# A later start of the weight rounding, with moved reciprocals, decay copies and buffers, in a fused attention and feed-forward kernel

## The chip, the cores and the metric

The kernel runs on one core of a Trainium2 chip. The metric is the device time of one execution in microseconds (us). The core has five engines that run side by side, each with its own in-order queue: TensorE (PE) for matrix products, VectorE (DVE), ScalarE (ACT) and GpSimd (POOL) for elementwise work, and SyncE (SP), which here issues nearly all of the DMA transfers. An instruction that waits holds up everything behind it on its own engine.

## The reference

The reference is an attention with a decay and a causal mask, followed by a feed-forward layer. B = 8 batches, H = 8 heads, S = 576 positions, D = 64 values per head, model width 512, hidden width 2048.

```python
scores = scale * np.matmul(q, k.transpose(0, 1, 3, 2))
cum = np.cumsum(np.log(np.clip(f, 0.0001, 1.0)), axis=-1)
scores = np.where(causal, -1e9, scores + cum[:, :, :, None] - cum[:, :, None, :])
attn = np.exp(scores - np.max(scores, axis=-1, keepdims=True))
attn = attn / (np.sum(attn, axis=-1, keepdims=True) + 1e-09)
x = np.matmul(attn, v)              # then heads are laid side by side: [4608, 512]
h = x @ w_in                        # [512, 2048]
g = np.maximum(h, 0.0) + alpha * np.minimum(h, 0.0)
out = g @ w_out                     # [2048, 512]
```

All of it is in fp32. The kernel splits each factor of a product into a rounded high part and a rest, and takes three products for one.

## The kernel before

**Attention** goes by pairs of heads: 32 pairs, n = 0 to 31, four to a batch. For each pair PE multiplies the query and key parts (`stretch`, and `tail` for the last 64 rows), DVE adds the decay rows `Z` and takes the row minimum (L744, L620), ACT takes the exponential and the row sum (L579), the result is transposed, and PE multiplies it with the values (`values`, `prods_of`).

- Pairs 0 to 9 transpose on PE (L592) and move the result out of PSUM with `evac` (L587 on DVE, L588 on ACT).
- Pairs 10 to 31 are **turned**: DVE transposes 32x32 blocks from the buffer `E` into `M` (L754), and sixteen DMAs (L764, ten issued by SP and six by POOL) carry them into the buffer `TT`, from which the value product reads. There are two `M` buffers and one `TT` buffer, so the DMAs of a pair can start only when the value product of the pair before has read `TT`. The value product of a pair runs two pairs late (`behind`). In the profile's names `TT` is a part of the tile `wr`, and `E` and `M` are parts of the tile `big`.
- For a turned pair, DVE spreads the decay into `Z` (L483), POOL copies parts of it to two more places (L501 and L502, two of each to a pair) and adds the mask (L504). POOL also makes the rests of query and key (L538).
- `rqk` holds the raw query and key rows, loaded by SP (L471, or L474 and L475) and read by ACT (L537) and POOL (L538). Up to pair 10 it has two buffers; the turned pairs after that use a ring `rqk1` with one.
- `quotients` turns the row sums into reciprocals: ACT adds a small number (L670), DVE takes the reciprocal (L671), PE transposes (L673), ACT copies (L674), SP writes them to DRAM (`rd`, L679) and fetches them back spread over partitions (`ri`, L686). They multiply the value product (L844), after which x is rounded (L846) and its rest taken (L848).

**The first feed-forward product** (`ffn1`, L362 with `xx,wi`) needs x of a whole batch and the rounded first weight `wi`. That weight is rounded in 16 pieces by `split64`: loads (L343), ACT (L345, L357), DVE (L348, L349, L352, L353), POOL (L358). Its products fill the time on PE between the steps of attention. **The second** (`w_out`) runs alone at the end as a seven-product scheme.

**The order** on every engine is written out by a small list scheduler, `Plan`, at build time. Each operation has an engine, an estimated duration, a key and the buffers it needs; of those that could start first the one with the smallest key is taken. The first product's operations have keys around 1e6, so that they come where nothing of attention can start. Up to 75 us of the plan, a gap on PE of over 0.5 us is filled with products whose result nobody reads (`fill`, L456). `CONV0` and `CONV` give the keys of the 16 weight pieces: `CONV0 + CONV * fc`, where pair n has the keys around `10 * n`.

## Time and profile before

| | |
|---|---|
| median of 3 runs | 1046.42 us (1045.65 to 1049.57) |
| the profiled execution, its own time | 1045.14 us |
| its span, first to last instruction | 1043.3 us |
| mean granted TensorE clock | 0.995 |
| PE busy | 1028.2 us of the span |
| DVE, ACT, POOL busy | 802.0, 631.2, 403.8 us |

Busy time of PE is the union of its matrix products, with their ends modelled; products follow each other faster than one takes, so a count and a stretch of time tell more than the duration of one. "Idle before" an instruction is put down to the engine or the DMA whose signal came last. The granted clock is given as a share of the full one.

### The profile page before, as it was taken

What the parts mean: (1) busy time and instruction counts of PE and PEld (TensorE: products, weight loads), DVE (VectorE), ACT (ScalarE), POOL (GpSimd) and SP (SyncE); (2) the same over time, 40 slices, a digit from 0 to 9 for tenths busy, and PEclk for the clock granted to TensorE, in tenths of its full rate; (3) what the DMA queues carried; (4) which work ended last, traced back from release to release, by engine and by line L of the source; (5) the groups of instructions that cost most, each with busy time, mean ns of one, the idle gap of its engine ahead of it and who ended that gap; (6) DMA issues with size and microseconds to landing.
All of it is one profiled execution on the core that took longest, in us unless ns stands there. A gap on an engine that the chain in (4) does not pass through costs nothing.

```text
span 1043.3 us, 22505 instructions
## 1 busy us (share of the span) xinstructions
PE 1028.2 (99%) x7994; PEld 899.7 (86%) x7994; DVE 802.0 (77%) x1702; ACT 631.2 (61%) x1462; POOL 403.8 (39%) x719
## 2 busy tenths in 40 slices
PE   9999999998999999999999999999999999999998
PEld 5888888787887787887888888899999999999998
DVE  5786885886776776767742987599898888989994
ACT  6779896675666666656552665655464545546551
POOL 6487674878887888886641000000000000000000
PEclk9999999998999999999999999999999999999999
DMA  5876754676888778886776666463434335344411
GB/s 173 236 224 209 231 171 131 195 218 180 254 236 224 233 225 229 245 242 183 213 207 194 213 222 203 166 201 121 140 123 140 122 122 161 117 129 139 124 62 41
DMA packets 125230, 187.74 MB, mean 180 GB/s; under 512 B 20967, under 2 KB 70622, under 8 KB 125118
## 3 DMA queue, kind: packets, MB, share of 16 engines
q1 hardware_dynamic: 120606, 173.13, 54.6%
q0 software_dynamic: 4224, 12.98, 4.8%
q8 instruction: 63, 1.03, 0.4%
q14 instruction: 49, 0.40, 0.1%
q10 hardware_dynamic: 288, 0.20, 0.1%
HBM read 102.80 MB, written 48.52 MB: 145 GB/s over the span
## 4 chain that ended last, share of the span: by engine, by line
PE 88%; POOL 4%; DMA 3%; DVE 2%; SPq 1%; issue 1%; ACT 1%; DVEq 0%; ACTq 0%; POOLq 0%
PE bank L362 84%; PE bank L592 2%; DMA rqk<-in_qk_dram 2%; SPq L764 1%; POOL Z L504 1%; PE bank L422 1%; POOL Ql L538 1%; POOL Kl L538 0%; DMA rd<-R 0%; PE bank L632 0%; DMA hd<-hs 0%; DVE big L744 0%; PE bank L456 0%; POOL xs L844 0%; POOL Z L510 0%
## 5 line engine op out<-in xcount | busy, mean ns | idle before, releaser
L362 PE MATMUL bank<-xx,wi 128*128 128x512 f32 x1728 | 418.2, 395 | 0.7 <-ACT eT L633 0.7
L362 PEld LDWEIGHTS bank<-xx,wi 128*128 128x128 f32 x1728 | 317.6, 188 | 74.1 <-issue 3.8
L579 ACT ACTIVATE big<-big,st 128x384 f32<-128x384 f32 (+4 forms) x268 | 156.1, 585 | 16.6 <-DVE st L744 15.1
L930 DVE SCALAR_TENSOR_TENSOR hs<-bank,sa,hs 128x512 f32<-128x512 f32 x96 | 71.7, 747 | 93.3 <-ACT hs L928 93.0
L362 PE MATMUL bank<-wot,xx 128*128 128x256 f32 x1008 | 123.9, 283 | 0.0
L362 PE MATMUL bank<-wi,xx 128*128 128x256 f32 x1008 | 123.9, 283 | 0.0
L362 PEld LDWEIGHTS bank<-wot,xx 128*128 128x128 f32 x1008 | 122.3, 192 | 0.0
L362 PEld LDWEIGHTS bank<-wi,xx 128*128 128x128 f32 x1008 | 122.3, 192 | 0.0
L744 DVE CUSTOM_DVE_ANT_0 big<-bank,Z 128x384 f32<-128x384 f32 (+3 forms) x211 | 92.9, 485 | 31.0 <-PE bank L362 22.9
L928 ACT ACTIVATE hs<-bank,ab 128x512 f32<-128x512 f32 x96 | 65.9, 686 | 82.5 <-PE bank L362 76.2
L754 DVE STREAM_TRANSPOSE big<-big 128x1152 f32<-128x1152 f32 (+1 forms) x66 | 79.3, 1221 | 13.6 <-ACT big L579 11.3
L764 POOL DMA_DIRECT2D wr<-big x132 | 66.4, 508 | 44.1 <-PE bank L632 24.7
L362 PE MATMUL bank<-wr,vr 128*64 128x128 f32 (+1 forms) x1232 | 68.3, 266 | 6.0 <-DMA wr<-big 4.2
L362 PEld LDWEIGHTS bank<-wr,vr 128*64 128x64 f32 x1232 | 60.1, 141 | 13.7 <-issue 6.9
L504 POOL TENSOR_TENSOR Z<-Z,tri 128x128 f32<-128x128 f32 x176 | 70.7, 428 | 0.0
L1153 ACT ACTIVATE xx<-gx 128x1024 fp32r<-128x1024 f32 x48 | 50.8, 1058 | 30.7 <-PE bank L362 15.1
L848 POOL TENSOR_TENSOR xx<-xs,xx 128x256 fp32r<-128x256 f32 x64 | 48.1, 764 | 49.4 <-ACT xx L846 49.0
L1156 DVE TENSOR_TENSOR xx<-gx,xx 128x1024 fp32r<-128x1024 f32 x48 | 58.5, 1218 | 7.9 <-ACT xx L1153 7.9
L362 PE MATMUL bank<-wi,gh 128*128 128x256 f32 x504 | 62.4, 283 | 0.0
L362 PE MATMUL bank<-wot,gh 128*128 128x256 f32 x504 | 62.4, 283 | 0.0
L362 PEld LDWEIGHTS bank<-wot,gh 128*128 128x128 f32 x504 | 61.4, 192 | 0.1
L362 PEld LDWEIGHTS bank<-wi,gh 128*128 128x128 f32 x504 | 61.3, 192 | 0.0
(157 smaller groups left out, 1749.4 us busy)
## 6 DMA issues: line engine op xcount, KB each, us to landing
hd<-hs SPq DMA_DIRECT2D x144, 256.0 KB
wx<-hd SPq DMA_DIRECT2D x47, 512.0 KB
wr<-big SPq DMA_DIRECT2D x220, 96.0 KB
rqk<-in_qk_dram SPq DMA_DIRECT2D x28, 512.0 KB
hr<-hd SPq DMA_DIRECT2D x25, 512.0 KB
wr<-big POOLq DMA_DIRECT2D x132, 96.0 KB, 3.7
vr<-in_vv_dram SPq DMA_DIRECT2D x32, 320.0 KB
wr<-in_w_in_dram SPq DMA_DIRECT2D x16, 512.0 KB
```

Source lines behind the costliest of these rows:

```text
L362: pe.matmul(o, lhsT, rhs, start=start, stop=stop)
L504: ms.append(op("POOL", c_po(128), lambda to=to, i=i, zd=zd: po.tensor_tensor(to()[:, :, -1:], zd()[:, :, i : i + 1], tk(), ALU.add), kc + ...
L579: ex = op("ACT", c_exp(w), lambda: ac.activation(at(bt.t), at(bt.t), AF.Exp, bias=lo()[:, col : col + 1], scale=-1.0, accum_out=su()[:, co ...
L592: pe.transpose(t[:, c : c + 128], src[:, 128 * j : 128 * j + 128], ident)
L744: ve.tensor_tensor_reduce(out=o if turned else blk(o), in0=blk(bS.t[:, c0 : c0 + w]), in1=in1(), scale=-0.125, scalar=3.0e38, op0=ALU.add, ...
L754: ve.transpose(part(bm.t), part(bE.t))
L764: got.append(op(e_, 600, lambda a=a, k=k, q_=q_: q_.dma_start(bTT.t[32 * k : 32 * k + 32, 768 * a : 768 * a + 768], bm.t[32 * a : 32 * a + ...
L848: xl = op("POOL", c_po(256), lambda r=r, t0=t0: po.tensor_tensor(bx.t[:, 1, t0 : t0 + 256], bxs[r].t[:, 0:256], bx.t[:, 0, t0 : t0 + 256]. ...
L928: cp = op("ACT", c_act(512), lambda bh=bh, bs=bs, fc=fc: ac.activation(bs.t, bh.t, AF.Relu, scale=ab[:, fc : fc + 1]), -1000, [last, o_sg] ...
L930: cp = op("DVE", c_dve(512), lambda bh=bh, bs=bs, fc=fc: ve.scalar_tensor_tensor(bs.t, bh.t, sa[:, fc : fc + 1], bs.t, ALU.mult, ALU.add), ...
L1153: his.append(op("ACT", c_acs(128 * GW * (j1 - j0)), lambda j0=j0, j1=j1, src=src, o_=o_: ac.activation(o_(0, j0, j1), src(), AF.Copy), key ...
L1156: rdy.append(op("DVE", c_dve(128 * GW * (j1 - j0)), lambda j0=j0, j1=j1, src=src, o_=o_: ve.tensor_tensor(o_(1, j0, j1), src(), o_(0, j0, ...
```

## The change

- `CONV0, CONV` go from 30, 2.2 to 40, 2.0: the keys of the weight pieces go from 30 ... 63 to 40 ... 70.
- `quotients` of turned pairs gets a key that is 20 smaller, so that its steps go ahead of others that could start at the same time.
- The two copies L501 and L502 go from POOL to ACT for the turned pairs: 44 of each.
- `rqk` keeps two buffers to the end; `rqk1` is gone.
- The memory of `TT` and of one `M` buffer is exchanged: `TT` lies in `big` now, and one of the two `M` buffers in `wr`. The counts stay the same.
- A second copy of the decay table in DRAM, `c8p`, is written by five DMAs on SP. It would be read by turned pairs that fetch their decay by DMA; with NZ = NX[0] = 10 there is none, so nothing reads it.
- `PJ` names the same three of eight DMAs for POOL as before, and `2 * NZ` and `NZ` are the same numbers as `2 * NX[0]` and `NX[0]`.

```diff
@@ -41,4 +41,5 @@
 LAG = 1000
+PJ = (2, 4, 6)
 VK, TK = 0.65, 5
-CONV0, CONV = 30, 2.2
+CONV0, CONV = 40, 2.0
 NW = NF // 2
@@ -227,2 +228,3 @@
     c8 = dram.tile([B * H, S], F32, name="c8")
+    c8p = dram.tile([B * H, S], F32, name="c8p")
 
@@ -264,3 +266,3 @@
     qkt = [sp.tile([128, QW + S], F32, name=f"rqk{i}") for i in range(2)]
-    rqk, rqk1 = Ring(Store(qkt)), Ring(Store([]))
+    rqk = Ring(Store(qkt))
     rZ = Ring(Store([(sp.tile([128, 2, ZW], F32, name=f"Z{i}"), sp.tile([128, S], F32, name=f"Zt{i}")) for i in range(2)]))
@@ -282,3 +284,3 @@
     cl = wf[0 : B * H, 0:S]
-    G0 = 2 * NX[0]
+    G0 = 2 * NZ
     GN = B * H - G0
@@ -391,2 +393,5 @@
     o_c8 = op("SP", 400, lambda: sy.dma_start(c8, ft()), -49, o_8, [bft], kb=147)
+    o_c8p = [op("SP", 400, lambda k=k: sy.dma_start(c8p[:, 128 * k : 128 * k + 128].rearrange("p (s c) -> p s c", c=32),
+                                                    c8[:, 0:512].rearrange("p (s k c) -> p s k c", k=4, c=32)[:, :, k]), 6, [o_c8], kb=60) for k in range(4)]
+    o_c8p.append(op("SP", 400, lambda: sy.dma_start(c8p[:, 512:S], c8[:, 512:S]), 6, [o_c8], kb=16))
     o_id = op("POOL", 600, lambda: make_identity(nc, ident), -98)
@@ -465,3 +470,3 @@
         kl, kc, bh = NS * n - 16, NS * n - 7, b * H + 2 * p
-        bqk, bZ = Buf(rqk1 if n > NX[0] else rqk), Buf(rZ)
+        bqk, bZ = Buf(rqk), Buf(rZ)
         q_, k_ = (lambda: bqk.t[:, 0:QW]), (lambda: bqk.t[:, QW : QW + S])
@@ -494,4 +499,5 @@
             else:
-                got = [op("SP", 400, lambda h=h: sy.dma_start(Z()[:, h, 0:512], c8[bh + h : bh + h + 1, 0:512].broadcast_to([128, 512])),
-                          kl + 1, [o_c8], [bZ], kb=256)]
+                c8_, o_ = (c8p, o_c8p) if n >= NX[0] else (c8, [o_c8])
+                got = [op("SP", 400, lambda h=h, c8_=c8_: sy.dma_start(Z()[:, h, 0:512], c8_[bh + h : bh + h + 1, 0:512].broadcast_to([128, 512])),
+                          kl + 1, o_, [bZ], kb=256)]
             if n >= NX[0]:
@@ -500,4 +506,4 @@
                 za, tk = (lambda zp=zp: zp(1152, 1280, 1)), (lambda: tri.rearrange("p (k s c) -> p k s c", s=1, c=32))
-                ms = [op("POOL", c_po(256) / 2, lambda zc=zc, zd=zd: po.tensor_copy(zc()[:, :, 0:2], zd()[:, :, 0:2]), kc + 0.1, got, [bZ]),
-                      op("POOL", c_po(128) / 2, lambda zb=zb, zd=zd: po.tensor_copy(zb()[:, :, 0:1], zd()[:, :, 0:1]), kc + 0.2, got, [bZ])]
+                ms = [op("ACT", c_acs(256), lambda zc=zc, zd=zd: ac.activation(zc()[:, :, 0:2], zd()[:, :, 0:2], AF.Copy), kc + 0.1, got, [bZ]),
+                      op("ACT", c_acs(128), lambda zb=zb, zd=zd: ac.activation(zb()[:, :, 0:1], zd()[:, :, 0:1], AF.Copy), kc + 0.2, got, [bZ])]
                 for to, i in ((zc, 2), (zb, 1), (za, 0), (zd, 3)):
@@ -527,3 +533,3 @@
         else:
-            tz = [op("SP", 400, lambda h=h: sy.dma_start(Zt()[64 * h : 64 * h + 64], c8[bh + h : bh + h + 1].broadcast_to([64, S])), kl + 1, [o_c8], [bZ], kb=147) for h in range(2)]
+            tz = [op("SP", 400, lambda h=h, c8_=c8_: sy.dma_start(Zt()[64 * h : 64 * h + 64], c8_[bh + h : bh + h + 1].broadcast_to([64, S])), kl + 1, o_, [bZ], kb=147) for h in range(2)]
         rt = op("POOL", 260, lambda: po.tensor_tensor(Zt()[:, 512:576], Zt()[:, 512:576], tri2, ALU.add), kc + 0.3, tz + [o_mask], [bZ])
@@ -762,3 +768,3 @@
                         a, k = j // 4, j % 4
-                        q_, e_ = ((sy, "SP"), (po, "POOL"))[j % 8 in (2, 4, 6)]
+                        q_, e_ = ((sy, "SP"), (po, "POOL"))[j % 8 in PJ]
                         got.append(op(e_, 600, lambda a=a, k=k, q_=q_: q_.dma_start(
@@ -886,3 +892,3 @@
                 waiting.pop()
-            quotients(k0 + 11 - hurry)
+            quotients(k0 + 11 - hurry - 20 * turned)
         later_x.append(rest)
@@ -955,3 +961,3 @@
     o_qc = [op("SP", 400, lambda a=a, c=c: sy.dma_start(c[32 * a : 32 * a + 32], c[0:32]), kc_ + 2, o_tc, kb=128) for a in range(1, 4) for c in (cq, cq2)]
-    o_cq = op("-", 0, lambda: rTT.store.items.append(wf[:, 0:3072]) or rTT.store.free.append((plan.t, 0)), 0, o_tc + o_qc)
+    o_cq = op("-", 0, lambda: rM.store.free.append((plan.t, len(rM.store.items))) or rM.store.items.append(wf[:, 0:3072]), 0, o_tc + o_qc)
 
@@ -959,3 +965,3 @@
         for c, s0 in ((cq, 0), (cq2, 16)):
-            po.tensor_copy(ct[64 * h : 64 * h + 64, s0 : s0 + c.shape[1], NX[0] :], c[64 * h : 64 * h + 64, :, h:GN:2])
+            po.tensor_copy(ct[64 * h : 64 * h + 64, s0 : s0 + c.shape[1], NZ:], c[64 * h : 64 * h + 64, :, h:GN:2])
 
@@ -963,3 +969,3 @@
     def swap():
-        for st, t in [(rE.store, big[:, 0:EW]), (rM.store, big[:, EW : EW + 3072]), (rM.store, big[:, EW + 3072 :]), (rqk1.store, qkt[0])]:
+        for st, t in [(rE.store, big[:, 0:EW]), (rM.store, big[:, EW : EW + 3072]), (rTT.store, big[:, EW + 3072 :])]:
             st.free.append((plan.t, len(st.items)))
```

The arithmetic is the same, and so is the number of products of attention and of both layers. What moves is the order. Three places matter below. Lines are numbered up to six higher after the change (L362 is L364, L456 is L461, L764 is L770).

**PE and DVE in pairs 2 and 3**, about 43 to 50 us into the execution before. On PE before, from the fill products around the transposes of pair 2 to its value product (`vr`):

```order
L456 MATMUL bank_76<-ident 128x128 x5
L592 MATMUL bank_76<-ident,big 128x128 x4
L592 MATMUL bank_80<-ident,big 128x128 x4
L456 MATMUL bank_83<-ident 128x128 x14
L362 MATMUL bank_78<-big,vr 64x128 x14
L362 MATMUL bank_78<-big,vr 64x64 x8
L362 MATMUL bank_78<-eT_0_110,vr 64x64 x2
```

and now:

```order
L461 MATMUL bank_77<-ident 128x128 x5
L598 MATMUL bank_77<-ident,big 128x128 x4
L598 MATMUL bank_81<-ident,big 128x128 x4
L364 MATMUL bank_84<-rqk_103 128x512
L364 MATMUL bank_79<-rqk_103 128x512
L461 MATMUL bank_83<-ident 128x128 x3
L364 MATMUL bank_77<-big,vr 64x128 x14
L364 MATMUL bank_77<-big,vr 64x64 x8
L364 MATMUL bank_77<-eT_0_111,vr 64x64 x2
```

In place of fourteen fill products stand two score products of pair 3 and three fill products. In the whole program there were 55 fill products, and there are 24.

On DVE at the same place before (L587 moves pair 2's transposed block out of PSUM, L348 to L353 round the second weight piece):

```order
L587 COPY big<-bank_76 128x4x128
L348 TENSOR_SCALAR wr<-wr 128x512
L349 SCALAR_TENSOR_TENSOR wr<-wr 128x512
L587 COPY big<-bank_80 128x4x128
L671 RECIPROCAL st_114<-st_114 128x9
L844 TENSOR_TENSOR xs_1_116<-xs_1_116,ri_119 128x256
L844 TENSOR_TENSOR xs_1_118<-xs_1_118,ri_119 128x320
L352 SCALAR_TENSOR_TENSOR wr<-wr 128x512
```

and now:

```order
L593 COPY big<-bank_77 128x4x128
L626 ISA big,st_113<-bank_78,Zt_107,st_113 128x320
L626 ISA st_113 128x1
L593 COPY big<-bank_81 128x4x128
L677 RECIPROCAL st_115<-st_115 128x9
L750 ISA big,st_113<-bank_82,Z_106 128x384
...
L350 TENSOR_SCALAR wr<-wr 128x512
L351 SCALAR_TENSOR_TENSOR wr<-wr 128x512
L354 SCALAR_TENSOR_TENSOR wr<-wr 128x512
L355 SCALAR_TENSOR_TENSOR wr<-wi,wr 128x512
L593 COPY big<-bank_77 128x4x64 x2
L677 RECIPROCAL st_113<-st_113 128x9
```

The rounding of the second piece stood between and behind the two moves of pair 2; it stands behind all of pair 3's row minima now. Up to the value product of pair 3, one piece less is rounded.

**PE between two turned value products.** Before, from the value product of pair 11 (its last row is the first here) to that of pair 12 (the last row here); `xx,wi` are products of the first layer, six to a row of `x6`, and left out between are score products:

```order
L362 MATMUL bank_80<-wr,vr 64x128 x6
L362 MATMUL bank_79<-Kh_99,Qh_97 128x128
...
L632 MATMUL bank_78<-ident,big 64x128
L362 MATMUL bank_76<-xx,wi 128x512 x6
L362 MATMUL bank_77<-xx,wi 128x512 x6
L362 MATMUL bank_82<-Kh_95,Qh_93 128x384
...
L362 MATMUL bank_79<-xx,wi 128x512 x6
L362 MATMUL bank_81<-Kh_95,Qh_93 128x256
...
L673 MATMUL bank_83<-ident,st_114 18x128
L362 MATMUL bank_78<-wr,vr 64x128 x14
```

and now:

```order
L364 MATMUL bank_77<-big,vr 64x128 x6
L364 MATMUL bank_82<-Kh_100,Qh_98 128x128
...
L364 MATMUL bank_80<-xx,wi 128x512 x6
L638 MATMUL bank_83<-ident,big 64x128
L364 MATMUL bank_81<-xx,wi 128x512 x6
L364 MATMUL bank_79<-xx,wi 128x512 x6
L364 MATMUL bank_84<-Kh_96,Qh_94 128x384
...
L364 MATMUL bank_80<-xx,wi 128x512 x6
L364 MATMUL bank_81<-xx,wi 128x512 x6
L679 MATMUL bank_78<-ident,st_115 18x128
L364 MATMUL bank_79<-xx,wi 128x512 x6
...
L364 MATMUL bank_83<-big,vr 64x128 x14
```

The first layer's products between these two went from 18 to 42 (six of them stand between the left-out rows). Over all turned pairs from 11 to 29, the counts between two value products were 18 once, 30 three times and 36 or more otherwise; now the smallest is 30, three times.

**SP in the turned pairs**, a round with reciprocals (`rd` is written, then `ri` is read back) and the ten DMAs into `TT` (L764). Before:

```order
L474 DMA rqk_101<-in_qk_dram 128x2x512
L475 DMA rqk_101<-in_qk_dram 128x192
L932 DMA hd<-hs 128x512 x2
L679 DMA rd_64<-R_120 18x128
L764 DMA wr<-big 32x768 x10
L932 DMA hd<-hs 128x512
L686 DMA ri_119<-rd_64 64x576
L686 DMA ri_119<-rd_64 64x64
L686 DMA ri_119<-rd_64 64x512
L558 DMA vr<-in_vv_dram 128x640
L474 DMA rqk_101<-in_qk_dram 128x2x512
```

and now:

```order
L479 DMA rqk_103<-in_qk_dram 128x2x512
L480 DMA rqk_103<-in_qk_dram 128x192
L685 DMA rd_65<-R_122 18x128
L938 DMA hd<-hs 128x512 x2
L692 DMA ri_120<-rd_65 64x576
L692 DMA ri_120<-rd_65 64x64
L692 DMA ri_120<-rd_65 64x512
L770 DMA big<-wr 32x768 x4
L938 DMA hd<-hs 128x512
L770 DMA big<-wr 32x768 x6
L564 DMA vr<-in_vv_dram 128x640
```

The three fetches of `ri` came behind the ten DMAs; now they come ahead of them, right behind the write of `rd`.

## The prediction

> **What bounds the kernel now.** I read the page first, for the shares of the engines:
>
> ```profile
> span 1043.3 us, 22505 instructions
> PE 1028.2 (99%) x7994; PEld 899.7 (86%) x7994; DVE 802.0 (77%) x1702; ACT 631.2 (61%) x1462; POOL 403.8 (39%) x719
> ```
>
> PE is the bound, with 15.1 us idle. The change leaves all needed products in place, so a gain can come from three things alone: idle time on PE, a lowered clock, and fill products that nobody reads. The second view is therefore the list of who PE waited for (engine, line, whom it waited for, us in total, times, the longest):
>
> ```profile
> PE bank L362 <- DMA wr<-big: 4.2, 2, 3.6
> PE bank L362 <- DVE st L620: 2.5, 3, 1.1
> PE bank L422 <- DVE wr L419: 1.5, 1, 1.5
> PE bank L362 <- ACT xs L831: 0.9, 1, 0.9
> PE bank L362 <- ACT eT L633: 0.7, 1, 0.7
> PE bank L592 <- DVE st L744: 0.7, 1, 0.7
> PE bank L673 <- DVE st L744: 0.4, 1, 0.4
> PE bank L362 <- DMA hd<-hs: 0.4, 1, 0.4
> ```
>
> These are 11.3 us, and the change can't reach the 1.5 us of L422, which is the start. Third, the timeline of PE, for where the two longest lie and what stands ahead of them (start, us, what; in brackets the idle time before):
>
> ```profile
> 45.19 3.29 PE L456 MATMUL bank<-ident 128*128 128x128 f32 x28
> ...
> 67.65 3.54 PE L362 MATMUL bank<-big,vr 128*64 128x128 f32 x44 [1.09 <-DVE st L620]
> ...
> 228.00 1.75 PE L362 MATMUL bank<-wr,vr 128*64 128x128 f32 x28
> ...
> 238.52 0.27 PE L673 MATMUL bank<-ident,st 128*18 128x128 f32 x1
> 242.44 3.26 PE L362 MATMUL bank<-wr,vr 128*64 128x128 f32 x28 [3.65 <-DMA wr<-big]
> ```
>
> One is at pair 3's value product, behind stretches of fill; the other at pair 12's, which waits for the DMAs into `TT`. Fourth, busy time by short stretches around both, for the clock (stretch, its length, busy of PE, then of PEld, DVE, ACT and POOL in the first two rows, granted clock, DMA share, GB/s):
>
> ```profile
> 66.00:68.00 2.00, 0.91 (x10) 0.59 (x10) 2.00 (x6) 1.78 (x4) 2.00 (x4) 0.75 0.95 282
> 68.00:70.00 2.00, 2.00 (x22) 2.00 (x20) 2.00 (x9) 1.31 (x4) 2.00 (x4) 0.50 0.97 337
> ...
> 242.00:244.00 2.00, 1.56 (x16) 0.50 0.86 312
> 244.00:246.00 2.00, 2.00 (x27) 0.50 0.47 155
> 246.00:248.00 2.00, 2.00 (x28) 0.53 0.00 0
> ```
>
> A stall costs more than its idle time here. After the 1.09 us the clock fell: about 0.5 us lost of the first stretch and 1.0 of the second, 1.5 us. After the 3.65 us it was 0.8, 1.0 and 0.9, 2.7 us. So the first place costs 2.6 us and the second 6.35 us, apart from the fill.
>
> [...]
>
> **The change part by part.** The sum is made against the profiled execution's own 1045.1 us; the median of the runs is 1.3 us above it, which I add at the end.
>
> *Weight pieces later (pairs 2 to 3).* 31 of 55 fill products go. One shows as two instructions in the trace, and this row is all of them:
>
> ```profile
> L456 PE MATMUL bank<-ident 128*128 128x128 f32 x110 | 14.3, 279 | 0.0
> ```
>
> In the long run of fill 28 instructions took 3.29 us, 0.235 us to a product, so 31 are 7.3 us. That is not yet a gain: the fill stood where PE had nothing else, and if DVE, which PE waits for there, is no earlier, idle time takes its place. What DVE does less before pair 3's value product:
>
> ```profile
> 46.02 2.06 DVE L349 SCALAR_TENSOR_TENSOR wr<-wr 128x512 uint32<-128x512 uint32 x1
> ...
> 62.85 0.43 DVE L348 TENSOR_SCALAR wr<-wr 128x512 uint32<-128x512 uint32 x1 [0.26 <-POOL wi L358]
> 63.32 0.69 DVE L349 SCALAR_TENSOR_TENSOR wr<-wr 128x512 uint32<-128x512 uint32 x1
> 64.04 0.69 DVE L352 SCALAR_TENSOR_TENSOR wr<-wr 128x512 uint32<-128x512 uint32 x1
> 64.77 1.28 DVE L353 SCALAR_TENSOR_TENSOR wr<-wi,wr 128x512 f32<-128x512 f32 x1
> 65.98 1.14 DVE L844 TENSOR_TENSOR xs<-xs,ri 128x256 f32<-128x256 f32 x2
> ```
>
> One piece of four instructions is 2.9 us (started apart as in these rows: 62.85 to 65.98 is 3.1 us), and one pair of x products, 1.1 us, also falls behind it: 4.0 us. Beside POOL's work L349 took 2.06 us once; that one no longer stands ahead of pair 2's value product, and I count it inside the 4 us. Useful PE work up to pair 3's value product is the same in both orders, so this place ends about 4.0 us sooner, and of the 7.3 + 1.1 us some 4 come back as idle time. Bounds: all of it gone, 7.3 + 2.6 = 9.9 us gained; or DVE no earlier, everything idle in two stalls with 2.7 us of clock each against 1.5 now, 3.9 us lost. I take 3.6 us, between the ends by DVE's rows.
>
> The pieces that come later are done in pairs 4 to 9 beside ACT's work. There is cover, though not much:
>
> ```profile
> 72.00:169.00 97.00, 97.00 (x796) 80.02 (x796) 71.51 (x167) 85.30 (x229) 60.33 (x74) 1.00 0.63 191
> 212.00:557.00 345.00, 336.80 (x2748) 272.46 (x2750) 239.39 (x570) 212.89 (x588) 256.68 (x477) 0.99 0.78 223
> ```
>
> In the first stretch PE never rests and ACT is busy 85.3 of 97 us (the fourth busy number). Between pair 3's value product and pair 9's the order has 18 first-layer products fewer (216 before, 198 now), and by the row
>
> ```profile
> 580.00:600.00 20.00, 20.00 (x90) 16.57 (x89) 18.55 (x32) 13.87 (x23) 1.62 (x2) 1.00 0.65 219
> ```
>
> one is 20 / 90 = 0.222 us, so PE asks for the same attention in 4.0 us less: ACT would be busy 85.3 of 93. It fits without a price; if it does not, the 4 us stand as idle time (a rival below).
>
> *The order of turned pairs.* Between the value products of pairs 11 and 12 PE had 18 first-layer products and was done at 238.8, 10.8 us after 228.00, while `TT` was full at 242.44: from one value product to the next the DMAs need 14.4 us. Six more products add 1.33 us: with 30 of them PE has 13.5 us of work, with 36 14.8, with 42 16.1. The count of 18 is gone (42 now), so the 6.35 us go too, since 16.1 is over 14.4. Three counts of 30 stay as there were three; two of these stalled before:
>
> ```profile
> 324.49 1.75 PE L362 MATMUL bank<-wr,vr 128*64 128x128 f32 x28 [0.70 <-DVE st L620]
> 388.98 1.75 PE L362 MATMUL bank<-wr,vr 128*64 128x128 f32 x28 [0.56 <-DMA wr<-big]
> ```
>
> Bounds: 6.35 us, and 0 if another pair takes the stall over. I take 6.3, because no count below 30 is left.
>
> *The other waits of the turned stage* sum to 11.3 - 1.5 - 1.1 - 3.65 - 0.7 (the start's L744, which stays) = 4.3 us. Two buffers of `rqk`, the early reciprocals and a lighter POOL work on what leads to them. How long ACT waits for `rqk` now, and the price of the moved copies (the last row is the nearest one on ACT):
>
> ```profile
> ACT Qh L537 <- DMA rqk<-in_qk_dram: 14.9, 5, 6.9
> L501 POOL COPY Z<-Z 128x256 f32<-128x256 f32 x44 | 17.4, 394 | 3.3 <-DVE Z L483 3.3
> L502 POOL COPY Z<-Z 128x128 f32<-128x128 f32 x44 | 11.6, 291 | 0.0
> L846 ACT ACTIVATE xx<-xs 128x256 fp32r<-128x256 f32 x64 | 24.9, 411 | 13.2 <-POOL xs L844 8.0 <-DVE xs L844 3.3 <-PE bank L362 1.4
> ```
>
> POOL loses 29.0 us. ACT gets at most 88 x 0.411 = 36 us, and has room: 212.9 of 345 us becomes 249 of 345, 72%. Lost cover would mean exponentials held behind a copy that waits for L483; POOL waited so once in 44 times, 3.3 us. I take half of the 4.3 us, 2.1; bounds 0 and 4.3.
>
> *What may be late next.* The early fetches of `ri` wait for `rd` to land, and now the ten DMAs into `TT` stand behind them on SP:
>
> ```profile
> 307.75 4.41 DMA rd<-R
> SPq L686 <- DMA rd<-R: 9.3, 3, 3.5
> ```
>
> The cover is the value product, since these DMAs can't start before it has read `TT`. From the transpose L673 the order has 12 to 18 first-layer products (2.7 to 4.0 us), a few score products (0.8) and the value product (3.0, 228.00 to 231) until then: 6.5 to 7.8 us. The chain is 0.3 + some 2 for ACT's copy + 0.3 + 4.4 = 7.0 us. So it just fits, with up to 0.5 us left over in some of eleven rounds.
>
> *The rest.* The five writes of `c8p` stand ahead of pair 2's `rqk` on SP:
>
> ```profile
> 10.43 1.35 SPq L528 DMA_DIRECT2D Zt<-c  x2
> 16.44 0.81 SPq L471 DMA_DIRECT2D rqk<-in_qk_dram  x2
> ```
>
> SP is free from 11.8 to 16.4 us; five at 0.68 (as L528) are 3.4 us: hidden, and without the cover 3.4 us at most. The exchange of `TT` and `M` keeps the counts: 0; so do `PJ` and `NZ`.
>
> For stalls that a new order brings with it I set 3.0 us, one like that at 67 us with its clock (2.6) and some tenths, and keep 0 to 7.8 (three) for the range. **Sum**: 1045.1 - 3.6 - 6.3 - 2.1 + 3.0 = 1036.1 us, and with the 1.3 us 1037.4: I say 1037.
>
> **The rivals.**
>
> (a) *The fill turns into idle time*, since ACT, at 85 of 97 us, or DVE sets the pace of pairs 2 to 9; only the turned stage gains: 1046.4 - 6.3 - 2.1 + 3.0 = 1041. For it: fill covered real waits. Against: DVE has a piece less there.
>
> (b) *Everything comes*: 9.9 + 6.3 + 4.3 us and no new stall: 1026. Against it: pair 3's value product would have to come 8.4 us earlier, and DVE is freed for 4.0.
>
> (c) *The stall moves*: another pair takes over the 6.35 us, and the early part is worth its 3.6 less 3.0: 1046. For it: `TT` is still single, and 36 products leave 14.8 against 14.4 us.
>
> (d) *Slower: SP is held by `rd`*. If reciprocals come so late that L673's result is not out before the value product ends, SP waits with the ten DMAs behind it, by the row above 3.1 us each time. With 36 products PE has 0.4 us to spare, so 2.7 us are lost in each of eleven rounds, 30 us: 1046.4 - 12.0 + 30 = 1064. It makes the kernel slower from about 2 us a round (11 x 1.6 = 18 us against gains of 12). For it: the chain of 7.0 us against a cover of 6.5 to 7.8. Against: the smaller key lets the sums' reciprocals go first.
>
> **How the numbers follow.** Forecast (1031 to 1041): 0.46; (a) 0.20; (b) 0.10; (c) 0.12; (d) 0.12. A measurement of this kernel can tell about 0.5%, 5.2 us, from no change, so faster means under 1041.2: the forecast, (b) and two thirds of (a), 0.69; same: the rest of (a) and most of (c), 0.18; slower: (d) and a bit of (c), 0.13. The range 1029 to 1047 leaves out (d), most of (b) and a part of (c).
>
> **What would show it.** Right: PE has no wait of over 1 us for `TT`'s DMAs between pairs 10 and 31, and no half clock around 240 us; pair 3's value product starts near 64 us instead of 67.65; L456 is near 48 instructions; ACT waits for `rqk` under 5 us; busy PE falls by about the fill, to 1021. Wrong: waits of PE for DVE or ACT between 45 and 70 us of more than 5 us (a); one new row of over 3 us in PE's waits (c); SP's L692 waiting for `rd` ten times or so, with `TT`'s DMAs late behind it (d). I am wrong altogether if pairs 4 to 9 stall for rounded weights.

## The result, and the profile after

The changed kernel takes 1039.56 us (median of 15 runs, 1037.89 to 1042.32) against 1045.88 us of the kernel before beside it: a ratio of 0.9949 with a 95% interval from 0.9934 to 0.9963. It is faster by about 0.5%, and the interval leaves out no change at all. The profiled execution took 1040.1 us, 5.0 us less than the one before. The page, first the span and the busy times:

```profile
span 1038.3 us, 22384 instructions
PE 1019.9 (98%) x7932; PEld 890.4 (86%) x7932; DVE 804.4 (77%) x1702; ACT 654.6 (63%) x1550; POOL 380.5 (37%) x631
```

PE is busy 8.3 us less, and the span is only 5.0 us shorter: PE's idle time grew from 15.1 to 18.4 us. Whom PE waited for (us in total, times, the longest):

```profile
PE bank L364 <- DVE st L626: 4.4, 2, 4.2
PE bank L598 <- ACT big L594: 2.0, 2, 1.7
PE bank L364 <- DVE hs L936: 1.8, 1, 1.8
...
PE bank L364 <- ACT eT L797: 1.0, 1, 1.0
PE bank L598 <- DVE big L593: 0.9, 1, 0.9
PE bank L598 <- ACT big L585: 0.8, 2, 0.4
...
PE bank L364 <- DMA big<-wr: 0.6, 1, 0.6
PE bank L364 <- DMA hd<-hs: 0.5, 1, 0.5
```

The wait of 3.65 us for `TT`'s DMAs is gone (0.6 us is left of that kind), and a new one of 4.2 us for the minimum of the last rows (L626) heads the list. The timeline of PE says where (start, us, what; in brackets the idle time before):

```profile
56.21 0.66 PE L598 MATMUL bank<-ident,big 128*128 128x128 f32 x4 [0.86 <-DVE big L593]
65.07 4.03 PE L364 MATMUL bank<-big,vr 128*64 128x128 f32 x44 [4.21 <-DVE st L626]
76.97 0.65 PE L598 MATMUL bank<-ident,big 128*128 128x128 f32 x4 [1.70 <-ACT big L594]
...
169.96 2.21 PE L364 MATMUL bank<-big,vr 128*64 128x128 f32 x44
...
248.11 1.75 PE L364 MATMUL bank<-big,vr 128*64 128x128 f32 x28
...
325.71 1.75 PE L364 MATMUL bank<-big,vr 128*64 128x128 f32 x28 [1.81 <-DVE hs L936]
...
388.67 1.75 PE L364 MATMUL bank<-big,vr 128*64 128x128 f32 x28 [0.57 <-DMA big<-wr]
```

Two early waits stand where the fill was taken out: 56.21 is a transpose and 65.07 pair 3's value product. The third, 76.97, is a transpose behind it, ahead of pair 4's. Pair 12's at 248.11 has no idle time before it. The clock around both places (stretch, its length, busy PE, PEld, DVE, ACT and POOL, granted clock, DMA share, GB/s):

```profile
62.00:64.00 2.00, 0.00 (x0) 0.00 (x0) 1.86 (x3) 0.00 (x0) 2.00 (x3) 0.51 0.80 275
64.00:66.00 2.00, 0.93 (x10) 0.94 (x12) 2.00 (x6) 1.39 (x3) 2.00 (x5) 0.50 1.01 219
66.00:68.00 2.00, 2.00 (x22) 2.00 (x20) 1.97 (x8) 0.00 (x0) 0.94 (x2) 0.50 0.74 210
68.00:70.00 2.00, 2.00 (x33) 1.68 (x30) 1.59 (x4) 0.52 (x2) 0.00 (x0) 0.78 0.00 0
...
240.00:260.00 20.00, 20.00 (x157) 16.02 (x157) 14.76 (x35) 14.76 (x43) 15.72 (x26) 1.00 0.83 234
```

and the last stretch in the kernel before:

```profile
240.00:260.00 20.00, 17.56 (x127) 14.50 (x127) 11.93 (x27) 11.21 (x32) 15.81 (x35) 0.83 0.63 178
```

The later place has its full clock back. The early one runs at half clock from 62 us, about 1.2 us into the wait, until about 69 us.

**A ledger by value products** shows where the 5.0 us come from. For each pair I take the time of its value product, credit 0.222 us for each first-layer product done by then (the row of the prediction), and write the lead over the kernel before. Pair 0 comes up to 0.9 us earlier or later in the executions profiled here, kernels with the same early order among them, so its own lead is taken off.

| lead over the kernel before, us, at pair | 3 | 4 | 9 | 11 | 13 | 31 |
|---|---|---|---|---|---|---|
| the change | +3.5 | -0.7 | -2.8 | -2.8 | +3.4 | +6.6 |
| the change, a second profile | +3.3 | -1.5 | -2.2 | -2.3 | +2.7 | +2.4 |

With -0.9 us ahead of pair 0 and -0.7 us behind pair 31 the first row gives the 5.0 us. Up to pair 3 there is a gain, up to pair 9 more than that is lost, and the turned stage gains 6.2 us between pairs 11 and 13 and 3.2 us behind that. The second profile lost 2.6 us again by pair 17, in a wait of 3.24 us for L936 at 327.98 us with slow products behind it (20 took 2.40 us, where 28 take 1.75 at the full clock), and ends with -0.3 us behind pair 13: single profiles of one program differ by that much, so below the medians decide, and the ledger only says where. The profile of the kernel before has such a loss in it, too: five of the kernels profiled here have its order up to pair 3 (it, a_conv30, c_late, b_early and c_pool), and the two that kept their clock there, b_early and c_pool (44 products of pair 3's value product in 2.21 us, for 3.54 before), stand at +1.3 us from pair 4 to pair 9.

### The profile page after: what moved, and what is told of

Same layout as the page of the kernel before. It is cut to its first block, busy times and chain, and to the rows that moved or that the text cites. A ratio compares the mean times of both kernels' runs of the same rounds, so it can differ in the third digit from the quotient of the medians.

```text
span 1038.3 us, 22384 instructions
## 1 busy us (share of the span) xinstructions
PE 1019.9 (98%) x7932; PEld 890.4 (86%) x7932; DVE 804.4 (77%) x1702; ACT 654.6 (63%) x1550; POOL 380.5 (37%) x631
## 4 chain that ended last, share of the span: by engine, by line
PE 86%; DVE 4%; DMA 3%; POOL 3%; ACT 2%; issue 1%; SPq 1%; DVEq 0%; POOLq 0%; ACTq 0%
PE bank L364 83%; DMA wr<-in_w_in_dram 2%; PE bank L598 1%; PE bank L427 1%; DVE wr L354 1%; ACT big L585 1%; POOL wi L360 1%; DVE wr L355 1%; SPq L770 1%; POOL Z L516 0%; ACT wi L359 0%; DVE wr L350 0%; DVE wr L351 0%; DMA ri<-rd 0%; DMA rd<-R 0%
## 5 line engine op out<-in xcount | busy, mean ns | idle before, releaser
L364 PE MATMUL bank<-xx,wi 128*128 128x512 f32 x1728 | 419.4, 396 | 1.0 <-ACT eT L797 1.0
L364 PEld LDWEIGHTS bank<-xx,wi 128*128 128x128 f32 x1728 | 317.1, 188 | 76.0 <-issue 6.7
L936 DVE SCALAR_TENSOR_TENSOR hs<-bank,sa,hs 128x512 f32<-128x512 f32 x96 | 71.9, 749 | 94.5 <-ACT hs L934 94.5
L364 PE MATMUL bank<-wot,xx 128*128 128x256 f32 x1008 | 123.9, 283 | 0.0
L364 PE MATMUL bank<-wi,xx 128*128 128x256 f32 x1008 | 123.9, 283 | 0.0
L364 PEld LDWEIGHTS bank<-wi,xx 128*128 128x128 f32 x1008 | 122.3, 192 | 0.0
L364 PEld LDWEIGHTS bank<-wot,xx 128*128 128x128 f32 x1008 | 122.3, 192 | 0.0
L364 PE MATMUL bank<-big,vr 128*64 128x128 f32 (+2 forms) x1752 | 97.4, 265 | 7.3 <-DVE st L626 4.4
L364 PEld LDWEIGHTS bank<-big,vr 128*64 128x64 f32 x1752 | 85.3, 139 | 17.7 <-DVE st L626 7.8
L510 POOL TENSOR_TENSOR Z<-Z,tri 128x128 f32<-128x128 f32 x176 | 69.6, 425 | 1.4 <-DVE Z L488 1.2
L364 PE MATMUL bank<-wot,gh 128*128 128x256 f32 x504 | 62.4, 283 | 0.0
L364 PE MATMUL bank<-wi,gh 128*128 128x256 f32 x504 | 62.4, 283 | 0.0
L364 PEld LDWEIGHTS bank<-wot,gh 128*128 128x128 f32 x504 | 61.4, 192 | 0.1
L364 PEld LDWEIGHTS bank<-wi,gh 128*128 128x128 f32 x504 | 61.3, 192 | 0.0
L364 PE MATMUL bank<-Kh,Qh 64*128 64x384 f32 (+3 forms) x280 | 59.8, 360 | 0.2 <-DVE st L750 0.2
L931 ACT ACTIVATE hs<-bank,sg 128x512 f32<-128x512 f32 x48 | 32.9, 686 | 34.2 <-PE bank L364 29.4
```

Source lines behind the costliest of these rows:

```text
L364: pe.matmul(o, lhsT, rhs, start=start, stop=stop)
L510: ms.append(op("POOL", c_po(128), lambda to=to, i=i, zd=zd: po.tensor_tensor(to()[:, :, -1:], zd()[:, :, i : i + 1], tk(), ALU.add), kc + ...
L931: cp = op("ACT", c_act(512), lambda bh=bh, bs=bs, fc=fc: ac.activation(bs.t, bh.t, AF.Copy, scale=sg[:, fc : fc + 1]), -1000, [last, o_sg] ...
L936: cp = op("DVE", c_dve(512), lambda bh=bh, bs=bs, fc=fc: ve.scalar_tensor_tensor(bs.t, bh.t, sa[:, fc : fc + 1], bs.t, ALU.mult, ALU.add), ...
```

## The experiments

Each is compared with runs of the kernel before on the same chip. The main ones take the change apart into three parts: the weight keys, the reciprocals' key, and the rest (copies on ACT, buffers, `c8p`). "Count" is the smallest number of first-layer products between two value products of turned pairs in the order.

| kernel | weight keys | reciprocals | the rest | fill products | count | ratio, 95% interval |
|---|---|---|---|---|---|---|
| before | 30, 2.2 | late | old | 55 | 18 | 1 |
| b_early | 30, 2.2 | early | old | 55 | 30 | 0.9906 (0.9883 to 0.9929) |
| c_late | 30, 2.2 | late | new | 55 | 30 | 0.9922 (0.9900 to 0.9945) |
| a_conv30 | 30, 2.2 | early | new | 55 | 30 | 0.9910 (0.9889 to 0.9931) |
| b_conv40 | 40, 2.0 | late | old | 24 | 18 | 0.9978 (0.9964 to 0.9992) |
| a_late | 40, 2.0 | late | new | 24 | 18 | 0.9982 (0.9968 to 0.9997) |
| b_both | 40, 2.0 | early | old | 24 | 30 | 0.9950 (0.9931 to 0.9968) |
| the change | 40, 2.0 | early | new | 24 | 30 | 0.9949 (0.9934 to 0.9963) |

**The change again**, for a second profile.

> The changed kernel itself once more, on the chip of the runs beside it, as the mark for them. All theories: a ratio of 0.995 to the kernel before, 1039 to 1040 us.

1041.79 us (7 runs), ratio 0.9959 (0.9945 to 0.9974). The result stands, and its spread from one set of runs to another is a tenth of a per cent.

**The change with the weight keys of before** (a_conv30), and **the kernel before with the new weight keys** (b_conv40):

```diff
-CONV0, CONV = 40, 2.0
+CONV0, CONV = 30, 2.2
```

> The changed kernel with the weight keys as before (30, 2.2) and all else as changed. Theory 1 (the later rounding loses 3.7 us up to pair 9, since a piece stands ahead of a row minimum that PE waits for; the gain is all in the turned stage): 1039.6 - 3.7 = 1035.9 us, pair 3's value product without a stall of over 2 us ahead of it, no half clock at 240 us. Theory 2 (the later rounding gains its 3.6 us as predicted, and it is the turned stage that gives less than forecast): 1039.6 + 3.6 = 1043.2 us.

> The kernel before with the later weight keys (40, 2.0) alone. The count of 18 first-layer products between pairs 11 and 12 stays in the order. Theory 1: 1045.9 + 3.7 = 1049.6 us, a stall of about 4 us ahead of pair 3's value product and the half clock at 240 us both there. Theory 2: 1045.9 - 3.6 = 1042.3 us.

a_conv30 took 1035.08 us (6 runs), ratio 0.9910: without the later weight pieces the change would have been about 0.4% faster, and the two intervals are just apart. b_conv40 took 1042.15 us (12 runs), ratio 0.9978, so alone the same edit gains a little. That is the time of theory 2 (theory 1 had 1049.6), but both stalls of theory 1 came. In its ledger it, too, loses by pair 9 (-1.4 us, after +3.5 at pair 3). It keeps the count of 18 and a wait of 2.72 us there, and it gains 5.5 us behind pair 13, where the new keys happen to give another order. What it gains isn't the fill.

**The reciprocals' key alone** on the kernel before (b_early), and the change **without it** (a_late):

```diff
-            quotients(k0 + 11 - hurry)
+            quotients(k0 + 11 - hurry - 20 * turned)
```

> The kernel before with the reciprocals' smaller key alone. The count of 18 first-layer products is gone from the order (42 and 30 follow in its place). Theory 1 (the turned stage gains by the counts, whatever lets the planner place them so): 1045 - 6.3 - some 2 of the other waits = 1036 to 1038 us. Rival (one rqk buffer and the loaded POOL still make the waits): the 6.3 us go, the other 4.3 us stay or grow, 1039 to 1041 us.

> The changed kernel with the reciprocals' keys as before. The order has 18 first-layer products between pairs 11 and 12 again, all else of the change is in. Theory 1 (that count makes the stall of 3.65 us and the clock's 2.7 us, whatever POOL and rqk do): 1039.6 + 6.3 = 1045.9 us, PE waits 3 to 4 us for the DMAs into TT there and the clock halves behind it. Theory 2 (a lighter POOL and two rqk buffers end that wait by themselves): 1039.6 us, no wait of over 1 us there.

b_early took 1034.98 us (6 runs), ratio 0.9906: this one key is worth more than the whole change. a_late took 1042.53 us (12 runs), ratio 0.9982, between its two theories. The count of 18 is back, and so is its stall, in the timeline of PE (the half clock behind it, too, 0.83 on the mean from 240 to 260 us):

```profile
244.66 3.25 PE L364 MATMUL bank<-big,vr 128*64 128x128 f32 x28 [3.79 <-DMA big<-big]
```

In the ledger it gains nothing between pairs 11 and 13, and 5.9 us behind that, so what the turned stage gains there doesn't need the early reciprocals.

**Only the rest** (c_late): the change with both keys as before. It tells whether it is the early reciprocals that gain, or the absence of the count of 18, whichever edit removes it.

```diff
-CONV0, CONV = 40, 2.0
+CONV0, CONV = 30, 2.2
-            quotients(k0 + 11 - hurry - 20 * turned)
+            quotients(k0 + 11 - hurry)
```

> The changed kernel without its two edits of keys: weight keys as before (30, 2.2) and the reciprocals' key as before. What is left are the copies on ACT, the two buffers of rqk to the end, the exchange of TT and M, and c8p. The order has all 55 fill products, and the smallest count of first-layer products between two turned value products is 30, so the count of 18 is gone without early reciprocals. Theory 1 (the count of 18 is what the gain was, whichever edit takes it away): no wait at pair 12, 6.3 us faster, ratio near 0.994. Theory 2 (early reciprocals work on the whole turned stage, and their 10 us are not only the count): the 6.3 us are partly taken back by other waits, ratio 0.997 to 1.000.

1037.04 us (6 runs), ratio 0.9922, where the count was expected to give 0.994 and the reciprocals' own work 0.997 to 1.000 without them. So the early reciprocals aren't needed: moving the copies and buffers reshuffles the order enough to lose the count of 18. Against a_conv30, which has them, no difference can be told. In the ledger the kernel gains 4.5 us between pairs 11 and 13 and 4.8 us behind that. Behind pair 13, eight of the thirteen profiles gain 3 to 6 us over the kernel before; the other five, with -2.5 to 1.5 us, each have a stall of 2 to 3.2 us of their own there (2.75 us in b_early, 3.24 us in the second profile of the change).

**Both keys without the rest** (b_both), the last of the eight combinations:

```diff
-CONV0, CONV = 30, 2.2
+CONV0, CONV = 40, 2.0
-            quotients(k0 + 11 - hurry)
+            quotients(k0 + 11 - hurry - 20 * turned)
```

> The kernel before with the two edits of keys alone: weight keys 40, 2.0 and early reciprocals; copies on POOL, one buffer of rqk, TT and M where they were. The order has 24 fill products. Theory 1 (the later weight keys take 4 to 5 us from the early reciprocals' 10 us, by PE's idle time in pairs 2 to 4): ratio 0.994 to 0.997, as the changed kernel. Theory 2 (the loss needs the moved copies or the second buffer of rqk): 0.989 to 0.992, as early reciprocals alone.

1039.89 us (11 runs), ratio 0.9950, the same as the change. The weight keys alone make the difference from b_early, 0.0044 of the time or 4.6 us (each against the runs of the kernel before beside it), and the rest adds nothing. Its wait ahead of pair 3's value product is even longer:

```profile
64.73 4.11 PE L362 MATMUL bank<-big,vr 128*64 128x128 f32 x44 [5.95 <-DVE st L620]
```

**The copies back on POOL**, in a_conv30 (c_pool):

```diff
-                ms = [op("ACT", c_acs(256), lambda zc=zc, zd=zd: ac.activation(zc()[:, :, 0:2], zd()[:, :, 0:2], AF.Copy), kc + 0.1, got, [bZ]),
+                ms = [op("POOL", c_po(256) / 2, lambda zc=zc, zd=zd: po.tensor_copy(zc()[:, :, 0:2], zd()[:, :, 0:2]), kc + 0.1, got, [bZ]),
```

and the second copy likewise.

> The changed kernel with the weight keys as before, and with the two decay copies back on POOL. Theory 1 (POOL has room, 257 of 345 us, and is not on the path): within 1.5 us of the 1035.1 us of the kernel without that step. Rival (the 29 us taken from POOL are what ends the other waits of the turned stage): 3 to 4 us more, 1038 to 1039 us.

1036.38 us (5 runs), ratio 0.9907 (0.9890 to 0.9924), against 0.9910 with the copies on ACT: no difference. In the change the copies cost ACT 26.9 us, with hardly a wait, by the groups of instructions (busy, mean ns, idle time before):

```profile
L507 ACT ACTIVATE Z<-Z 128x256 f32<-128x256 f32 x44 | 15.7, 405 | 0.4 <-DVE Z L488 0.4
L508 ACT ACTIVATE Z<-Z 128x128 f32<-128x128 f32 x44 | 11.2, 295 | 0.0
```

**Why the fill came back as idle time.** The timeline of DVE in the change ahead of pair 3's value product:

```profile
58.45 0.41 DVE L626 CUSTOM_DVE_ANT_0 big<-bank,Zt 128x256 f32<-128x256 f32 x1
...
59.45 1.62 DVE L350 TENSOR_SCALAR wr<-wr 128x512 uint32<-128x512 uint32 x1 [0.58 <-POOL wi L360]
61.11 1.28 DVE L351 SCALAR_TENSOR_TENSOR wr<-wr 128x512 uint32<-128x512 uint32 x1
62.43 1.28 DVE L354 SCALAR_TENSOR_TENSOR wr<-wr 128x512 uint32<-128x512 uint32 x1
63.81 0.73 DVE L355 SCALAR_TENSOR_TENSOR wr<-wi,wr 128x512 f32<-128x512 f32 x1
64.46 0.54 DVE L626 CUSTOM_DVE_ANT_0 big<-bank,Zt,st 128x320 f32<-128x320 f32 x1
...
67.11 0.42 DVE L350 TENSOR_SCALAR wr<-wr 128x512 uint32<-128x512 uint32 x1
67.56 0.69 DVE L351 SCALAR_TENSOR_TENSOR wr<-wr 128x512 uint32<-128x512 uint32 x1
```

The third weight piece stands between the two last minima, L626, and PE waits for the second. It first waits 0.58 us for POOL and then takes 5.1 us, with POOL at work beside it nearly throughout; two operations of the next piece (67.11 and 67.56), with POOL idle, need 0.42 and 0.69 us. Two kernels go at this piece. In a_dep2 it waits for that minimum too, by a dependency:

```diff
-        b1 = op("DVE", 1480, bits, key, [ld], [br, ba], two=True)
+        b1 = op("DVE", 1480, bits, key, [ld, *dve], [br, ba], two=True)
```

with `dve` the last minimum of pair 4 for the third piece and nothing for the others.

> The changed kernel, in which the third weight piece on DVE also waits for pair 4's last row minimum of the tail (L626), so that it stands behind it and not ahead. Theory 1: the idle 4.2 us ahead of pair 3's value product falls under 1 us and the clock's loss behind it goes, 1039.6 - 4.2 - 1.5 = about 1034 us. Theory 3 (ACT, at 85 of 97 us, sets the pace of pairs 2 to 9 and the piece only shows it): the stall moves to pair 4 or 5, 1039 to 1040 us.

In x_bits two of the four DVE operations of the pieces 2 to 5 are left out:

```diff
-            ve.scalar_tensor_tensor(a(), hi(), 0xC0000000, a(), ALU.bitwise_and, ALU.bitwise_or)
+            if not half:
+                ve.scalar_tensor_tensor(a(), hi(), 0xC0000000, a(), ALU.bitwise_and, ALU.bitwise_or)
```

and L354 likewise.

> The changed kernel; in weight pieces 2 to 5 two of the four DVE instructions (the sign bits and the low word) are left out, so eight DVE instructions fewer, with the order of all else the same. Theory 4 (DVE's work, slowed beside POOL, sets the time up to pair 4's value product): 2 to 4 us sooner at pair 3's value product (65.1 us now) and 6 us or more at pair 4's (85.2 us now), 1033 to 1035 us. Theory 3 (ACT sets that pace): pair 4's value product moves by under 2 us, 1038 to 1040 us.

a_dep2 took 1037.42 us (6 runs), ratio 0.9932 (0.9912 to 0.9951), between its two theories; x_bits 1038.83 us (6 runs), 0.9935 (0.9912 to 0.9959). Both intervals overlap with that of the change, so these ratios don't tell either from it. Beside the change's own second set on the same chip, though at another time, all six runs of a_dep2 (1035.94 to 1038.43) lie below all seven of the change (1040.03 to 1043.95); those of x_bits (1034.66 to 1042.48) don't.

The ledgers, one profile each, say more. Both bring pair 3's value product forward, by 3.8 and 3.1 us. Pair 4's comes at 83.61 us in a_dep2 (behind six more first-layer products) and at 82.69 us in x_bits, against 85.15 in the change and 83.57 before: 2.5 us sooner in x_bits, where the theories had 6 and under 2. At pair 9 they stand at +1.2 and +0.6 us, against -2.8 in the change, so 4.0 and 3.4 us of the early loss are gone and stay gone. Against the kernel before, though, most of the lead that they have at pair 3 (+7.3 and +6.6 us) is lost by pair 4 (+2.1 and +1.7), as it is in the change. In a_dep2 the wait of 4.2 us is gone, and five others of 4.8 us together (1.46, 1.18, 0.57, 0.55 and 1.04, for DVE and once for ACT) stand between the two. So the piece ahead of that minimum is the larger part of the loss, about 4 of 6.3 us, and not all of it: behind it PE is held by other steps of the same pairs.

**Other weight keys**: 36, 2.2 puts the third piece behind that minimum, with 34 fill products; 26, 2.4 leaves the second piece ahead of pair 3's last minimum, with 39.

```diff
-CONV0, CONV = 40, 2.0
+CONV0, CONV = 36, 2.2
```

> The changed kernel with weight keys 36, 2.2: 34 fill products, the second weight piece behind pair 3's minima as in the change, but the third one behind pair 4's last tail minimum, which PE waited 4.2 us for in the changed kernel. Theory 1 (that one piece in front of that minimum makes the loss): no such wait, ratio near 0.990. Theory 2 (DVE and POOL do the same work up to pair 5 in any of these orders, and what fill is taken out comes back as idle time): waits of 3 to 5 us somewhere in pairs 3 to 5, ratio 0.993 to 0.996.

> The changed kernel with weight keys 26, 2.4: 39 fill products, the second weight piece in front of pair 3's last tail minimum. Theory 2 (fill is only a cover, and the pace up to pair 5 is the same): pair 4's value product at 82 to 86 us, and a ratio between the changed kernel and that with keys 30, 2.2: 0.990 to 0.994. If the early pieces decide by themselves (each piece earlier lets a first-layer product take the place of fill), it is the fastest of all: under 0.989.

a_c36_22 took 1035.67 us (6 runs), ratio 0.9910 (0.9885 to 0.9935), as theory 1 had it; a_c26_24 1038.71 us (6 runs), 0.9934 (0.9912 to 0.9956), neither the fastest nor apart from the others. I had expected pair 4's value product at 82 to 86 us in any order; it comes at 88.58 us in a_c26_24, behind 48 first-layer products. The other kernel, a_c36_22, shows another way out, in its timeline of PE:

```profile
60.29 2.21 PE L364 MATMUL bank<-big,vr 128*64 128x128 f32 x44
...
74.06 2.09 PE L364 MATMUL bank<-xx,wi 128*128 128x512 f32 x8 [1.57 <-POOL xx L854]
...
88.50 1.75 PE L364 MATMUL bank<-big,vr 128*64 128x128 f32 x28
...
165.69 2.21 PE L364 MATMUL bank<-big,vr 128*64 128x128 f32 x44
```

Pair 4's value product comes late here, at 88.50 us. But by then 60 first-layer products are done, and in the change 24. What stood idle there is useful work here, so its lead is +8.1 us at pair 3, +3.8 at pair 4 and still +3.9 at pair 9. The stretch from 45 to 90 us in this kernel:

```profile
45.00:90.00 45.00, 43.37 (x387) 36.08 (x387) 37.48 (x87) 36.79 (x102) 36.73 (x44) 1.00 0.79 237
```

in the change:

```profile
45.00:90.00 45.00, 37.72 (x362) 31.12 (x361) 37.15 (x89) 34.23 (x101) 34.52 (x42) 0.92 0.75 214
```

and before:

```profile
45.00:90.00 45.00, 43.87 (x428) 37.29 (x426) 36.65 (x90) 34.93 (x97) 35.37 (x43) 0.96 0.73 215
```

DVE, ACT and POOL do about the same work in all three. In the change PE rests 7.3 us of this stretch, against 1.1 before, and the clock is lower. In a_c36_22 two things differ at once, the piece's place and the first-layer products at hand; and they weren't separated beyond a_dep2: with the piece alone behind the minimum, its lead at pair 9 is +1.2 us, which is 4.0 of the 6.7 us between a_c36_22 and the change.

## Why the prediction was right, and where it was not

The time (1037 predicted, 1039.56 measured), the sign and the range held. The way there held only in the turned stage, and there its size is sure for the count of 18 alone.

**The count of 18: right.** Predicted 6.3 us, and 0 if another pair took the stall over. The ledger shows 6.2 us between pairs 11 and 13, no half clock, and no stall of that kind elsewhere over 0.6 us. All kernels without the count gain 4.5 to 6.3 us there, and the two others with it 0 and 0.5. So rival (c), the moved stall, did not come; the sign named for it, a new row of over 3 us in PE's waits, did (L626, 4.4 us), but at pair 3 and not in a turned pair. I put the gain down to the order, and c_late shows that this was right whichever edit changes it.

**The other turned waits: the size is not settled.** Predicted 2.1 us, half of the 4.3 us listed; behind pair 13 the first profile has 3.2 us, with a new wait of 1.81 us (325.71) inside it, and the second -0.3 us. The orders a_conv30 and c_late have 4.2 and 4.8 us. Why the order before is the worst of them was not taken apart. Two of the reasons I named for it are worth nothing measurable: the copies (c_pool), and the second buffer of `rqk`. ACT's 14.9 us of waits for `rqk` are gone, and yet b_both, which has one buffer, is as fast as the change.

**Weight pieces later: this step failed.** Its first half came as worked out. 24 fill products are left, in 48 instructions,

```profile
L461 PE MATMUL bank<-ident 128*128 128x128 f32 x48 | 6.9, 284 | 0.0
```

PE waits 0.86 and 4.21 us where I expected some 4 us of idle time, and pair 3's value product has gained 3.5 us, where I set 3.6. What failed is the next sentence, "It fits without a price". I argued from ACT's busy share that pairs 4 to 9 would go faster once PE asked for less. They went 1.9 us faster from pair 4 to pair 9 (84.81 us for 86.68) with 4.0 us less asked of PE, and 4.2 us had gone before that, between pairs 3 and 4. Compare pair 9's value product at 169.96 us above with that of the kernel before:

```profile
170.25 1.97 PE L362 MATMUL bank<-big,vr 128*64 128x128 f32 x35
```

Ahead of it PE has 31 fill products (7.3 us) and 18 first-layer products (4.0 us) less to do, and it comes 0.3 us sooner (1.2 us, with the later start of this execution taken off). The work taken out came back as waits (76.97, 149.41, 155.0 and 164.81 us among them) and as a lower clock (0.92 from 45 to 90 us, for 0.96). That is rival (a), which I had at 0.20, and it is what happened: -2.8 us at pair 9 in place of +3.6. About 4 us of that is the third weight piece on DVE ahead of the minimum that PE waits for (a_dep2). That minimum kept a piece ahead of it, the third where the fourth stood (62.85 in the prediction's rows), and this one took 5.1 us where I had set 2.9 for a piece. The rest is waits of several kinds. Busy shares of 85 of 97 us said that ACT had room. They didn't say what each step waits for: in the change, too, no engine was full from 72 to 169 us (PE 92.9 of 97 us, ACT 85.6, DVE 72.7, POOL 65.6). That this rest is a chain of steps, each waiting for one on another engine, I read from the five waits of a_dep2; it was not measured link by link.

**New losses: 3.0 us set, 6.3 us came**, waits and clock together, all between pairs 3 and 9. So the sum was near for a wrong reason, which is luck: 3.6 - 3.0 = 0.6 us for the early part, where 3.5 - 6.3 = -2.8 us was measured, and the turned stage gave 9.4 us in the first profile (4.7 in the second) in place of 8.4. The 1.5 us of clock that the prediction books on pair 3's place are not a price of that place either: the same wait in the same order left the clock alone in b_early and c_pool (last section).

**Rival (d), SP held by `rd`**: its mechanism came, its price did not. SP's waits in the turned stage:

```profile
SPq L692 <- DMA rd<-R: 17.4, 8, 3.7
SPq L770 <- PE bank L364: 15.8, 12, 2.8
```

There were 3 waits of 9.3 us before, and there are 8 of 17.4 us. But only one value product waited for its DMAs (0.57 us, at 388.67), so the cover of 6.5 to 7.8 us was enough. b_early, with 6 such waits of 10.8 us, is among the fastest.

So of the signs I named, the fill, PE's busy time (1019.9 us for 1021), ACT's waits for `rqk` and the two of the turned stage were on the right side. Pair 3's value product was one us later than 64. PE's waits for DVE between 45 and 70 us are 5.07 us, just over the 5 us named as the sign of rival (a), and that sign was the true one.

## What to carry to other kernels

Filler work on a bound engine may cover a pace that is set elsewhere. Before it is counted as a gain, ask whether the next step that really ends the stretch (here pair 9's value product) comes earlier, and not only whether the other engines have free time; taking the cover away cost clock here as well (0.92 from 45 to 90 us in the change, 0.96 before). Look, too, at what stands ahead of the step that is waited for: one piece of weight rounding ahead of a row minimum cost about 4 us here. Where that piece stood behind the minimum and first-layer products stood in place of fill (a_c36_22), the lead stayed; which of the two kept it is in part open. And a change of several parts is best costed by what each part does to the order at the one place that stalls: here either of two edits that removed the count of 18 was worth 0.8 to 0.9% by itself, and the later weight pieces, which saved fill, gave nearly half of that back.

## What the runs showed of the hardware

**In these profiles the length of a wait doesn't tell whether the clock falls.** In c_late PE waits twice for L626:

```profile
68.63 3.58 PE L364 MATMUL bank<-big,vr 128*64 128x128 f32 x40 [1.10 <-DVE st L626]
...
241.73 1.75 PE L364 MATMUL bank<-big,vr 128*64 128x128 f32 x28 [1.58 <-DVE st L626]
```

and the stretches there are

```profile
68.00:70.00 2.00, 1.37 (x14) 1.37 (x16) 2.00 (x8) 1.40 (x5) 2.00 (x3) 0.57 1.00 321
...
242.00:244.00 2.00, 2.00 (x51) 2.00 (x48) 1.12 (x1) 0.85 (x3) 2.00 (x5) 1.00 1.03 363
```

The shorter wait, at pair 3, was followed by the half clock, as the one of 1.09 us was before the change; the longer one left it at full speed. The place doesn't decide it either. In b_early, with the same order up to there, the same wait left the clock at full:

```profile
67.04 2.21 PE L362 MATMUL bank<-big,vr 128*64 128x128 f32 x44 [1.10 <-DVE st L620]
...
68.00:70.00 2.00, 2.00 (x45) 1.68 (x39) 1.96 (x9) 1.25 (x3) 2.00 (x4) 1.00 0.97 326
```

In c_pool, too, the 44 products behind the same wait (1.09 us) took 2.21 us. Even one program differs. The wait of 1.70 us at 76.97 left the full clock in the first profile of the change (1.00 from 78 to 82 us), and in the second it didn't:

```profile
76.58 0.66 PE L598 MATMUL bank<-ident,big 128*128 128x128 f32 x4 [1.70 <-ACT big L594]
...
78.00:80.00 2.00, 2.00 (x15) 1.96 (x12) 1.93 (x3) 1.78 (x7) 2.00 (x3) 0.61 0.00 0
```

And in a_c26_24 the clock is low at pair 3 with no wait over 0.43 us in the ten us before:

```profile
64.12 4.11 PE L364 MATMUL bank<-big,vr 128*64 128x128 f32 x44
...
66.00:68.00 2.00, 2.00 (x30) 2.00 (x28) 1.97 (x5) 0.63 (x1) 2.00 (x5) 0.50 0.82 289
```

Behind seven of the longest waits the products were slow. The 28 products of a turned value product, 1.75 us at the full clock (248.11 in the change), took 3.26 us behind 3.65 us of waiting in the kernel before, 3.25 behind 3.79 in a_late, 3.16 behind 2.97 in a_c26_24 and 2.15 behind 3.16 in x_bits. The 44 of an early one, 2.21 us at the full clock (169.96 in the change), took 4.03 us behind 4.21 in the change and 4.11 behind 5.95 in b_both. Twelve first-layer products, 3.06 us at 311.01 us in b_early, took 5.14 there behind 2.75. In the kernel before and in the change's first profile the clock fell three times inside the kernel. It was at half for 3.4 us once (67.0 to 70.4 before the change) and for 6.8 us twice (241.1 to 247.9 there, 62.05 to 68.9 in the change). It fell 0.4 us into the wait of 1.09 us, 1.2 us into the one of 4.21 us, and 2.3 us into the one of 3.65 us, as the stretch from 241 us in the kernel before shows:

```profile
241.00:242.00 1.00, 0.00 (x0) 0.00 (x0) 0.00 (x0) 1.00 (x3) 1.00 (x3) 0.53 0.64 77
```

What decides was not tested.

**DVE beside POOL.** L350 in the timeline of DVE above took 1.62 us (59.45 to 61.07), against 0.42 us with POOL idle. POOL at that time:

```profile
59.38 1.41 POOL L544 TENSOR_TENSOR Kl<-rqk,Kh 128x576 fp32r<-128x576 f32 x1
60.76 2.40 POOL L516 TENSOR_TENSOR Z<-Z,tri 128x384 f32<-128x384 f32 x2
```

L350 ended 0.28 us after POOL's L544 (60.79), and L354 (62.43, 1.28 us) 0.55 us after the second L516 (63.16). With POOL idle L354 took 0.68 us (68.91), and L351, 1.28 us here, took 0.69 (67.56). Not every operation beside POOL is longer: L355 (63.81) took 0.73 us beside L517 and L518, against 0.69 with POOL idle (70.89). Why some are was not tested. I had priced a piece at 2.9 us, partly from a row beside POOL (L353 at 64.77, 1.28 us, beside L510 from 64.18 to 65.50; another took 0.69 us at 40.23 with POOL idle), and the one in front of PE took 5.1 us.
